# A gated-scan and GELU feed-forward kernel: the second GEMM with its weights stationary and its activations moving

## The chip, the cores and the metric

The kernel runs on one core of one Trainium2 chip. The metric is the device time of one execution in microseconds, smaller is better. Engines: TensorE (PE, its weight loads PEld), VectorE (DVE), ScalarE (ACT), GpSimd (POOL) and SyncE (SP, which here only issues transfers).

## The reference

An attention with a gated running state over 768 time steps for 4 batches of 8 heads of 48, then a feed-forward layer over the 3,072 tokens with 384 features and 2,048 hidden units, all in float32:

```python
for t in range(S):
    state = alpha[:, :, t, :, None] * state + np.einsum('bhd,bhe->bhde', k[:, :, t], v[:, :, t])
    y[:, :, t] = np.einsum('bhd,bhde->bhe', q[:, :, t], state)
...
h = x @ w_in
g = 0.5 * h * (1.0 + erf(h * inv_sqrt2))
return (g @ w_out).astype(np.float32)
```

Here x is y with the heads side by side, w_in is 384 x 2048 and w_out 2048 x 384.

## The kernel before, in words

The tokens are cut into 12 groups of 256 (`G`), three to a batch. For each group the attention part (lines 266 to 535: scans on VectorE, many small TensorE products) makes x transposed, 384 features in three tiles (`NK`) of 128 partitions by 256 tokens, split into a high half `xhi` and a low half `xlo` so that float32r products keep float32's accuracy. The weights are split in the same way (`wih`, `wil`, `woh`, `wol`).

The hidden units are cut into 8 pieces f of 2 x 128. One GEMM1 step (`gemm1`, line 545) makes one piece of one group: for each 128 hidden units j and each feature tile i three products (high by high, high by low, low by high), 18 products of 256 columns with the weights stationary and x moving, into one PSUM tile `hp` of 128 x 512. ScalarE then writes GELU(hp) twice, rounded to float32r as `ghi` (L576) and in full in place (L577), and VectorE writes the difference as `glo` (L582). One GEMM2 step (`gemm2`, line 594) multiplies them with the piece's w_out: for each token half t and each j `ghi` by `woh`, `ghi` by `wol` and `glo` by `woh`, 12 products. There the activations are stationary (a 128 x 128 tile of `ghi` or `glo`) and 384 columns of weights move, into two PSUM tiles `acc0` and `acc1` of 128 tokens x 384. GEMM2 of a piece stands behind GEMM1 of the next piece on TensorE. There are 96 steps of each kind.

After the last piece of a run `evacuate` brings the two accumulators to `part` in SBUF, on ScalarE (L620), VectorE (L622) or, where a group is taken up again, with an add on VectorE (L618). POOL's queue stores it to `out` (L628); the last group alone is stored in two halves from SP's and ScalarE's queues (L624).

The order of the instructions on TensorE, VectorE, ScalarE and SP is made in Python by a planner: a table of costs (`COST`, line 36) and rules give every operation a start, and the operations are then written in the order of the starts (lines 981 to 1022). In the first 380 us the GEMM steps stand between the small products of the attention part; after that there are only GEMM steps. `X_GAP`, `HI_GAP` and `LO_GAP` (line 35) are the sizes in bytes of unused tiles that shift where x, `ghi` and `glo` begin in SBUF.

Of the kernel before, what the change touches and what calls it, by code (L numbers as in the profile page):

```python
# [8 lines left out]
F32 = mybir.dt.float32  # L9
# [6 lines left out]
ALU = mybir.AluOpType  # L16
# [15 lines left out]
RATE, ALONE, LATENCY, SMALL, BEGIN = 350e3, 290e3, 2.1, 50e3, 2.2  # L32
MARGIN = 1.5
HOME = {0: 0, 1: 1, 2: 2, 4: 1, 5: 0, 6: 2, 8: 1, 9: 0, 10: 2, "s": 1}
X_GAP, Z_GAP, HI_GAP, LO_GAP, LATE_GAP = (128, 0, 192), 0, (64, 0), (0, 64), 0
COST = dict(
    scan=0.65, back=0.72, keys=0.65, q=1.35, qv=0.62, scores=1.0, kn=0.5, mask=0.62, inside=1.05, chain=1.15, outer=0.85, carry=0.26, last=0.34, last_p=0.15, sums=0.55, scaled=0.45,
    xh=0.6, xl=0.65, spread=0.62, check=0.95, load=0.46, fetch=0.46, u=0.92, c0=0.56, c1=0.9, c2=0.45, c3=0.95, c4=0.92,
# [6 lines left out]
def gla_then_gelu_ffn(ctx: ExitStack, tc: tile.TileContext, q, k, v, alpha, akq, w_in, w_out, out):  # L45
    nc = tc.nc
    B, H, D, S = q.shape
    NF, P, NK, _ = w_in.shape
    DM, DFF = NK * P, NF * P
    NT = B * S  # L50
    C = 128
    G = 2 * C
# [8 lines left out]
    NG = B * GPB  # L61
    NSB = GPB
# [4 lines left out]
    const = ctx.enter_context(tc.tile_pool(name="const", bufs=1))  # L67
# [5 lines left out]
    ps_o = ctx.enter_context(tc.tile_pool(name="ps_o", bufs=1, space=PSUM))  # L73
# [43 lines left out]
    for t in qk:  # L117
        for h in range(2):
            r = slice(h * DP, (h + 1) * DP)
# [15 lines left out]
    for half in range(2):  # L135
        r = slice(half * CS, (half + 1) * CS)
        nc.gpsimd.affine_select(
            out=mask[r],
# [10 lines left out]
    wi_hi, wi_lo, wo_hi, wo_lo = (  # L149
        [const.tile([P, 2, DM], F32R, name=f"{n}{f2}") for f2 in range(NF2)] for n in ("wih", "wil", "woh", "wol")  # L150
    )
# [28 lines left out]
    for f2 in range(NF2):  # L180
        src = w_in[2 * f2 : 2 * f2 + 2].rearrange("two p c f -> p two (c f)")
        pieces.append((src, wi_hi[f2], wi_lo[f2]))
        src = w_out[2 * f2 * P : (2 * f2 + 2) * P, :].rearrange("(two p) e -> p two e", p=P)
# [303 lines left out]
    def x_tiles(g):  # L487
        if g != "s" and g % (XB + 1) == XB:
            x = late[0].tile([P, NK, 2, G], F32R, tag="xl", name=f"x{g}")
            if g == XB:  # L490
                gap(late[0], LATE_GAP, "gap_late")
        else:
            if g in range(XB):
                gap(ffn, X_GAP[HOME[g]], f"gap_x{g}")
            x = ffn.tile([P, NK, 2, G], F32R, tag=f"x{HOME[g]}", bufs=1, name=f"x{g}")
        xt[g] = x[:, :, 0], x[:, :, 1]
        return x
# [94 lines left out]

        return out

    parts = [const.tile([P, 2, DM], F32, name=f"part{i}") for i in range(NSB)]
    started = set()

    def gemm2(g, f, ghi, glo, acc, first, last, done, n0=None):
        for k in range(2):
            for t in range(2):  # L600
                for j in range(2):
                    for a, w in (((ghi, wo_hi[f]), (ghi, wo_lo[f])), ((glo, wo_hi[f]),))[k]:
                        nc.tensor.matmul(  # L603
                            acc[t],
                            lhsT=a[:, j, t * C : (t + 1) * C],
                            rhs=w[:, j, :],
                            start=(first and j == 0 and k == 0 and w is wo_hi[f]),
                            stop=(last and j == 1 and k == 1),
                        )
        EARLY = tuple(range(NSB))  # L610
        if not last:
            return

        def evacuate():
            o = parts[0 if g == "s" else g % NSB]
            for t in range(2):
                if g in started:
                    nc.vector.tensor_tensor(out=o[:, t], in0=o[:, t], in1=acc[t], op=ALU.add)  # L618
                elif g in EARLY or t == 1 and g == NG - 1:
                    nc.scalar.copy(o[:, t], acc[t])  # L620
                else:
                    nc.vector.tensor_copy(o[:, t], acc[t])  # L622
                if g == NG - 1:
                    (nc.scalar if t else nc.sync).dma_start(out[g * G + t * C : g * G + (t + 1) * C, :], o[:, t])  # L624
            started.add(g)
            if done and g != NG - 1:
                rows = out[g * G : (g + 1) * G, :] if n0 is None else out[bass.ds(n0, G), :]
                nc.gpsimd.dma_start(rows.rearrange("(t p) e -> p t e", p=C), o)  # L628

        return evacuate  # L630

    def general_path():
# [6 lines left out]
        flat = [[x[:, n * NPAIR * G : (n + 1) * NPAIR * G] for n in range(3)] for x in both]  # L639
        st = flat[0][0][:, : DS * D].rearrange("p (d e) -> p d e", e=D)  # L640
# [13 lines left out]
        with tc.For_i(0, S, T) as t0:  # L654
# [20 lines left out]
            half = T * D // 2  # L675
            for i in range(2):
# [3 lines left out]
                    lhsT=sel,  # L680
                    rhs=yc.rearrange("p t e -> p (t e)")[:, i * half : (i + 1) * half],
                    start=True,
                    stop=True,
# [8 lines left out]
        with tc.For_i(0, NT, G) as n0:  # L692
            x_tiles("s")
            xhi, xlo = xt["s"]
            for c in range(2):
                y, z = flat[0][c][:, :DM], flat[1][c][:, :DM].rearrange("p (c h d) -> p c h d", c=NK, h=2)
                nc.sync.dma_start(y, out[bass.ds(n0 + c * C, C), :])
                main, rest = y[:, : NK * DD], y[:, NK * DD :]
                nc.vector.tensor_copy(z[..., :D], main.rearrange("p (c h d) -> p c h d", c=NK, h=2))
                nc.vector.tensor_copy(z[..., D:], rest.rearrange("p (h c d) -> p c h d", c=NK, h=2))  # L700
                xp = small_bank([P, NK, C], f"xp_s{c}")
                for i in range(NK):
                    nc.tensor.transpose(out=xp[:, i, :], in_=z[:, i].rearrange("p h d -> p (h d)"), identity=ident)
                e = slice(c * C, (c + 1) * C)
                nc.scalar.copy(xhi[:, :, e], xp)
                nc.vector.tensor_tensor(out=xlo[:, :, e], in0=xp, in1=xhi[:, :, e].bitcast(F32), op=ALU.subtract)
            acc = [ps_o.tile([P, DM], F32, tag=f"acc{t}", name=f"acc{t}_s") for t in range(2)]
            for f in range(NF2):
                hp = gemm1("s", f)
                gh = gelus("s", f, hp)  # L710
                gl = gelu_low("s", f, hp, gh)
                evacuate = gemm2("s", f, gh, gl, acc, f == 0, f == NF2 - 1, f == NF2 - 1, n0)
            evacuate()
# [180 lines left out]
    def gemm1_op(g, t):  # L894
        f = next_f[g]
        next_f[g] += 1
        st = dict(g=g, f=f, first=g != state["g"], last=False)
        prev = steps[-1] if steps else None
        if st["first"]:
            if prev:  # L900
                prev["last"] = True
                again = prev["g"] >= NSB or prev["g"] in evacuated
                evacuated.add(prev["g"])
                prev["evac"] = Op("DVE" if again else "ACT", "part", lambda p=prev: p["out"](), [prev["gemm2"]], rank=-2)
                waiting[prev["evac"].eng].append(prev["evac"])
            state["run"] += 1
        state["g"] = g
        two = steps[-2] if len(steps) > 1 else {}
        st["gemm1"] = Op("PE", "gemm1", lambda: st.update(hp=gemm1(g, f)))
        st["gelu"] = Op("ACT", "gelu", lambda: st.update(gh=gelus(g, f, st["hp"])), [st["gemm1"], two.get("gemm2")], rank=-3)  # L910
        st["gelu"].cost *= 2
        st["low"] = Op("DVE", "low", lambda: st.update(gl=gelu_low(g, f, st["hp"], st["gh"])), [st["gelu"], two.get("gemm2")], rank=-3)

        if g < NSB and t < UNTIL:
            st["minus"] = Op("PE", "minus", lambda: st.update(rest=gelu_rest(g, f, st["hp"], st["gh"])), [st["gelu"]], rank=-3)
            st["low"] = Op("ACT", "gelu", lambda: st.update(gl=st["rest"]()), [st["minus"], two.get("gemm2")], rank=-2.9)
            waiting["PE"].append(st["minus"])

        def second():
            if st["first"]:  # L920
                st["acc"] = [ps_o.tile([P, DM], F32, tag=f"acc{t}", name=f"acc{t}_{g}_{f}") for t in range(2)]
            else:
                st["acc"] = prev["acc"]
            st["out"] = gemm2(g, f, st["gh"], st["gl"], st["acc"], st["first"], st["last"], f == NF2 - 1)

        st["gemm2"] = Op("PE", "gemm2", second, [st["low"], prev and prev["gemm2"], prev and prev.get("evac")], rank=0)
        waiting["ACT"].append(st["gelu"])
        waiting[st["low"].eng].append(st["low"])
        gemms[g, f] = st["gemm1"]
        steps.append(st)  # L930
        return st["gemm1"]
# [49 lines left out]
    t = 0.0  # L981
    idle = 0
    while True:
        moved = False
        for e in ("DVE", "ACT", "PE", "SP", "POOL"):
            if free_at[e] <= t + 1e-9:
                o = choose(e, t)
# [11 lines left out]
    last = steps[-1]  # L999
# [9 lines left out]
    first = min(o.start for o in plan if o.name == "gemm1")  # L1009
    early = sorted((o for o in plan if o.eng == "PE" and o.start <= first), key=lambda o: o.start)  # L1010
    for o, after in zip(early, early[1:]):
        n = int((after.start - o.end - 0.3) / FILL)
# [18 lines left out]
    with tc.If(rv != 0):  # L1031
        general_path()
# [57 lines left out]
```

## Time and profile before

| | |
|---|---|
| median of 3 runs | 509.78 us (508.96 to 510.25) |
| profiled execution | 510.61 us |
| its span from the first to the last instruction | 509.0 us |
| mean granted TensorE clock | 0.995 |
| TensorE / VectorE / ScalarE / GpSimd busy | 495.7 / 297.3 / 219.6 / 39.1 us |

The profiled execution took 1.6 us more than its span, and 0.83 us more than the median of the runs. Busy time of TensorE counts a moment once where several products overlap, while the duration of a single product in the rows runs from its issue to its modelled end, so that durations of neighbours overlap; how fast products follow one another is read from their starts.

### The profile page before, as it was taken

Reading aid. Unit: us, or ns where it says so; the run is one execution under the profiler, and the core shown is the slowest. Engines: PE = TensorE matmul, PEld = TensorE weight load, DVE = VectorE, ACT = ScalarE, POOL = GpSimd, SP = SyncE. Lnnn points to the kernel's source line nnn. Section 1 sums busy time; section 2 is a strip of 40 time slices with the busy share of each in tenths; the row PEclk is TensorE's granted clock in tenths of the full one; section 3 lists DMA queues with packets and bytes.
Section 4 is the critical chain, followed back from the end, with each engine's and each line's share of the span. In section 5 each row is a group of like instructions: output and inputs, shape, how many; then the busy total and the mean of one; then the engine's idle time right before and its main releaser. Section 6 shows DMA issues by size and latency. Waiting matters only on the chain.

```text
span 509.0 us, 13811 instructions
## 1 busy us (share of the span) xinstructions
PE 495.7 (97%) x5974; PEld 477.0 (94%) x5974; DVE 297.3 (58%) x579; ACT 219.6 (43%) x468; POOL 39.1 (8%) x60
## 2 busy tenths in 40 slices
PE   8898999999999999999999999999999999999995
PEld 7787999999998999999999999999999999999995
DVE  6999899999849968667686267252332211211211
ACT  1676864645544455454453343353323222222221
POOL 4100110100011111121111011010000000000000
PEclk9998999999999999999999999999999999999999
DMA  8957453531033423433332020010000000000001
GB/s 301 381 176 237 184 172 125 186 127 63 1 125 111 136 73 108 133 112 118 109 100 77 0 68 14 1 35 15 1 35 14 0 33 2 32 0 1 32 1 35
DMA packets 15250, 44.20 MB, mean 87 GB/s; under 512 B 2224, under 2 KB 5728, under 8 KB 15184
## 3 DMA queue, kind: packets, MB, share of 16 engines
q1 hardware_dynamic: 13520, 38.44, 22.9%
q0 software_dynamic: 1232, 4.33, 2.2%
q8 instruction: 49, 0.80, 0.7%
q10 hardware_dynamic: 432, 0.49, 0.4%
q14 instruction: 17, 0.14, 0.1%
HBM read 36.18 MB, written 4.72 MB: 80 GB/s over the span
## 4 chain that ended last, share of the span: by engine, by line
PE 80%; issue 12%; ACT 2%; DVE 2%; DMA 2%; POOL 1%; SPq 0%; ACTq 0%; DVEq 0%; POOLq 0%
PE acc L603 34%; PE hp L555 33%; PE s L314 3%; PE ybank L470 3%; PE ybank L387 2%; PE ybank L409 2%; DMA st<-in_moe_w_in_dram 2%; PE spare L1007 1%; ACT junk L170 1%; PE ybank L355 1%; POOL qk L288 1%; PE ybank L533 0%; ACTq L547 0%; SPq L158 0%; ACT L576 0%
## 5 line engine op out<-in xcount | busy, mean ns | idle before, releaser
L555 PE MATMUL hp<-x,wih 128*128 128x256 f32 x1152 | 204.7, 280 | 0.0
L555 PEld LDWEIGHTS hp<-x,wih 128*128 128x128 f32 x1152 | 178.6, 189 | 1.9
L555 PE MATMUL hp<-x,wil 128*128 128x256 f32 x576 | 160.0, 278 | 0.0
L576 ACT ACTIVATE ghi<-hp 128x512 fp32r<-128x512 f32 x96 | 57.4, 598 | 204.8 <-PE hp L555 204.8
L582 DVE TENSOR_TENSOR glo<-hp,ghi 128x512 fp32r<-128x512 f32 x92 | 63.0, 685 | 141.0 <-ACT hp L577 140.9
L603 PE MATMUL acc<-woh,ghi 128*128 128x384 f32 x384 | 131.9, 344 | 0.0
L603 PE MATMUL acc<-wol,ghi 128*128 128x384 f32 x384 | 128.9, 336 | 0.0
L555 PEld LDWEIGHTS hp<-x,wil 128*128 128x128 f32 x576 | 108.9, 189 | 0.0
L603 PE MATMUL acc<-woh,glo 128*128 128x384 f32 x384 | 82.1, 334 | 0.0
L603 PEld LDWEIGHTS acc<-woh,ghi 128*128 128x128 f32 x384 | 72.0, 188 | 3.0
L603 PEld LDWEIGHTS acc<-wol,ghi 128*128 128x128 f32 x384 | 72.1, 188 | 0.0
L603 PEld LDWEIGHTS acc<-woh,glo 128*128 128x128 f32 x384 | 67.9, 188 | 0.0
L577 ACT ACTIVATE hp<-hp 128x512 f32<-128x512 f32 x96 | 56.9, 593 | 0.0
L278 DVE TENSOR_TENSOR_SCAN pp<-akq,top 128x256 f32<-128x256 f32 x48 | 31.3, 680 | 23.5 <-POOL qk L288 21.3
L293 DVE TENSOR_TENSOR_SCAN rp<-akq,rp,top 128x255 f32<-128x255 f32 x48 | 35.2, 762 | 0.7
L288 POOL TENSOR_TENSOR qk<-akq,pp 128x512 f32<-128x512 f32 x18 | 23.7, 1319 | 135.3 <-PE ybank L470 75.5
L628 POOL DMA_DIRECT2D out_dram<-part x11 | 8.4, 762 | 258.6 <-DVE part L622 188.5
L314 PE MATMUL s<-qk,akq 48*64 48x112 f32 x768 | 24.7, 261 | 1.6 <-issue 1.0
L524 ACT CAST x<-ybank 64x256 fp32r<-64x256 f32 (+4 forms) x60 | 20.0, 333 | 11.4 <-PE ybank L470 8.8
L528 DVE TENSOR_TENSOR x<-ybank,x 64x256 fp32r<-64x256 f32 (+3 forms) x54 | 19.2, 355 | 8.5 <-ACT x L524 7.6
L314 PEld LDWEIGHTS s<-qk,akq 48*64 48x64 f32 x768 | 19.4, 133 | 3.8 <-issue 2.8
L323 ACT COPY kn<-s 128x384 f32<-128x384 f32 x24 | 11.6, 482 | 25.0 <-PE s L314 18.1
(78 smaller groups left out, 405.6 us busy)
## 6 DMA issues: line engine op xcount, KB each, us to landing
akq<-in_akq_dram SPq DMA_DIRECT2D x22, 768.0 KB, 4.8
st<-in_moe_w_in_dram SPq DMA_DIRECT2D x8, 768.0 KB, 4.5
st<-in_moe_w_out_dram SPq DMA_DIRECT2D x8, 768.0 KB, 5.2
vn<-in_v_dram SPq DMA_DIRECT2D x12, 384.0 KB, 4.4
out_dram<-part POOLq DMA_DIRECT2D x11, 384.0 KB, 3.2
x<-z SPq DMA_DIRECT2D x63, 32.0 KB, 2.7
akq<-in_akq_dram SPq DMA_DIRECT2D x2, 512.0 KB, 5.5
akq<-in_akq_dram SPq DMA_DIRECT2D x2, 256.0 KB, 2.8
```

Source lines behind the costliest of these rows:

```text
L278: nc.vector.tensor_tensor_scan(pp[:, i], at[:, i], top, MID, ALU.mult, ALU.min)
L288: eng.tensor_tensor(out=qs[:, :, :, :CS], in0=by_chunk(qt), in1=by_chunk(pp), op=ALU.mult)
L293: nc.vector.tensor_tensor_scan(rp[:, i, G - 2 :: -1], at[:, i, G - 1 : 0 : -1], top[:, 1:], rp[:, i, G - 1 :], ALU.mult, ALU.min)
L314: nc.tensor.matmul(d["s"][o, h, e : e + KW], lhsT=d["kt"][r, i, t], rhs=d["qs"][r, i, j], start=True, stop=True)
L470: ins = nc.tensor.matmul(ybank[o, b, t : t + CS], lhsT=states[u][j][r, i], rhs=d["qs"][r, i, j, :CS], start=False, stop=True, skip_group_c ...
L524: nc.scalar.copy(hi, y)
L528: nc.vector.tensor_tensor(out=lo, in0=y, in1=hi.bitcast(F32), op=ALU.subtract)
L555: nc.tensor.matmul(hp[:, j, :], lhsT=a[:, j, i * P : (i + 1) * P], rhs=x[:, i, :], start=(j == 0 and i == 0 and n == 0), stop=(i == NK - 1 ...
L576: nc.scalar.activation(ghi, hp, AF.Gelu)
L577: nc.scalar.activation(hp, hp, AF.Gelu)
L582: nc.vector.tensor_tensor(out=glo, in0=hp, in1=ghi.bitcast(F32), op=ALU.subtract)
L603: nc.tensor.matmul(acc[t], lhsT=a[:, j, t * C : (t + 1) * C], rhs=w[:, j, :], start=(first and j == 0 and k == 0 and w is wo_hi[f]), stop= ...
```

## The change

GEMM2 swaps its operands. A 128 x 128 tile of w_out (`woh` or `wol`, output features i of 128) is now stationary and the 256 tokens of `ghi` or `glo` move, so that a step has 3 output tiles x 2 halves j x 3 terms = 18 products of 256 columns, and the result is transposed: output features on the partitions, tokens along the columns. The accumulators are one PSUM tile of 2 x 256 columns (`acc2`) and one of 256 (`acc1`). The evacuation moves 512 and then 256 columns. The output array holds each block of 256 tokens transposed; the program's last lines turn the blocks round on the host. In the very last step the products are ordered by accumulator, and the two accumulators are copied in halves by VectorE and ScalarE and stored in four transfers. Three gaps change: the x tiles and the weights stay where they were, `ghi` and `glo` begin 64 bytes lower. The planner's costs and rules are untouched.

```diff
-X_GAP, Z_GAP, HI_GAP, LO_GAP, LATE_GAP = (128, 0, 192), 0, (64, 0), (0, 64), 0
+X_GAP, Z_GAP, HI_GAP, LO_GAP, LATE_GAP = (128, 0, 256), 0, (0, 0), (0, 0), 0
...
-    parts = [const.tile([P, 2, DM], F32, name=f"part{i}") for i in range(NSB)]
+    parts = [const.tile([P, NK, G], F32, name=f"part{i}") for i in range(NSB)]
...
+    def accumulators(g, f):
+        return [ps_o.tile([P, n, G], F32, tag=f"acc{n}", name=f"acc{n}_{g}_{f}") for n in (2, NK - 2)]
+
+    def rows_of(start):
+        flat = out[start, :].rearrange("r c -> (r c)")
+        return flat.rearrange("(i p t) -> p i t", p=P, t=G)
+
     def gemm2(g, f, ghi, glo, acc, first, last, done, n0=None):
-        for k in range(2):
-            for t in range(2):
-                for j in range(2):
-                    for a, w in (((ghi, wo_hi[f]), (ghi, wo_lo[f])), ((glo, wo_hi[f]),))[k]:
-                        nc.tensor.matmul(
-                            acc[t],
-                            lhsT=a[:, j, t * C : (t + 1) * C],
-                            rhs=w[:, j, :],
-                            start=(first and j == 0 and k == 0 and w is wo_hi[f]),
-                            stop=(last and j == 1 and k == 1),
-                        )
+        final = done and g == NG - 1
+        terms = ((wo_hi[f], ghi, 0), (wo_lo[f], ghi, 0), (wo_hi[f], glo, 1))
+        todo = [(i, j, n) for i in range(NK) for j in range(2) for n in range(3)]
+        todo.sort(key=lambda x: (x[0] // 2 if final else 0, terms[x[2]][2], x[0], x[1], x[2]))
+        for i, j, n in todo:
+            w, a, k = terms[n]
+            nc.tensor.matmul(
+                acc[i // 2][:, i % 2],
+                lhsT=w[:, j, i * P : (i + 1) * P],
+                rhs=a[:, j, :],
+                start=(first and i % 2 == 0 and j == 0 and n == 0),
+                stop=(last and j == 1 and k == 1),
+                skip_group_check=True,
+            )
...
         def evacuate():
             o = parts[0 if g == "s" else g % NSB]
-            for t in range(2):
+            if final:
+                rows = rows_of(slice(g * G, (g + 1) * G))
+                for b, (i, n) in enumerate(((0, 2), (2, 1))):
+                    to, src = (x.rearrange("p i t -> p (i t)") for x in (o[:, i : i + n], acc[b]))
+                    half = n * G // 2
+                    for k in range(2):
+                        e = slice(k * half, (k + 1) * half)
+                        (nc.scalar.copy if k else nc.vector.tensor_copy)(to[:, e], src[:, e])
+                        at = rows[:, i + k] if n == 2 else rows[:, i, e]
+                        (nc.scalar if k else nc.sync).dma_start(at, to[:, e])
+                return
+            for a, to in zip(acc, (o[:, :2], o[:, 2:])):
                 if g in started:
-                    nc.vector.tensor_tensor(out=o[:, t], in0=o[:, t], in1=acc[t], op=ALU.add)
-                elif g in EARLY or t == 1 and g == NG - 1:
-                    nc.scalar.copy(o[:, t], acc[t])
+                    nc.vector.tensor_tensor(out=to, in0=to, in1=a, op=ALU.add)
+                elif g in EARLY:
+                    nc.scalar.copy(to, a)
                 else:
-                    nc.vector.tensor_copy(o[:, t], acc[t])
+                    nc.vector.tensor_copy(to, a)
...
+    o = got[0].reshape(-1, 384, 256)
+    return o.transpose(0, 2, 1).reshape(got[0].shape)
```

All steps keep their order on every engine; only what stands inside a GEMM2 step and inside an evacuation differs. First TensorE at a GEMM2 step in the last group (group 11, piece 6), behind the last GEMM1 step; a row is line, operation, output<-inputs and shape. Before, the whole step:

```order
L603 MATMUL acc0_11_0_6082<-woh6_160,ghi_11_6_6276 128x384
L603 MATMUL acc0_11_0_6082<-wol6_168,ghi_11_6_6276 128x384
L603 MATMUL acc0_11_0_6082<-woh6_160,ghi_11_6_6276 128x384
L603 MATMUL acc0_11_0_6082<-wol6_168,ghi_11_6_6276 128x384
L603 MATMUL acc1_11_0_6083<-woh6_160,ghi_11_6_6276 128x384
L603 MATMUL acc1_11_0_6083<-wol6_168,ghi_11_6_6276 128x384
L603 MATMUL acc1_11_0_6083<-woh6_160,ghi_11_6_6276 128x384
L603 MATMUL acc1_11_0_6083<-wol6_168,ghi_11_6_6276 128x384
L603 MATMUL acc0_11_0_6082<-woh6_160,glo_11_6_6279 128x384 x2
L603 MATMUL acc1_11_0_6083<-woh6_160,glo_11_6_6279 128x384 x2
```

And with the change, from the seventh product on (the six ahead of it are three more pairs of woh6 and wol6 into acc2):

```order
L612 MATMUL acc2_11_0_6608<-ghi_11_6_6838,woh6_160 128x256
L612 MATMUL acc2_11_0_6608<-ghi_11_6_6838,wol6_168 128x256
L612 MATMUL acc1_11_0_6609<-ghi_11_6_6838,woh6_160 128x256
L612 MATMUL acc1_11_0_6609<-ghi_11_6_6838,wol6_168 128x256
L612 MATMUL acc1_11_0_6609<-ghi_11_6_6838,woh6_160 128x256
L612 MATMUL acc1_11_0_6609<-ghi_11_6_6838,wol6_168 128x256
L612 MATMUL acc2_11_0_6608<-glo_11_6_6841,woh6_160 128x256 x4
L612 MATMUL acc1_11_0_6609<-glo_11_6_6841,woh6_160 128x256 x2
```

Both accumulators take their ghi products first and the glo products stand at the end of the step as before, now as the 13th to the 18th product.

The second place is the end of the program on ScalarE, behind the GELU of the last step. Before:

```order
L576 ACTIVATE ghi_11_6_6276<-hp_11_6_6245 128x512
L577 ACTIVATE hp_11_6_6245<-hp_11_6_6245 128x512
L576 ACTIVATE ghi_11_7_6312<-hp_11_7_6281 128x512
L577 ACTIVATE hp_11_7_6281<-hp_11_7_6281 128x512
L620 COPY part2_175<-acc1_11_0_6083 128x384
L624 DMA out_0_dram<-part2_175 128x384
```

And with the change:

```order
L576 ACTIVATE ghi_11_7_6880<-hp_11_7_6843 128x512
L577 ACTIVATE hp_11_7_6843<-hp_11_7_6843 128x512
L633 COPY part2_175<-acc2_11_0_6608 128x256
L635 DMA out_0_dram<-part2_175 128x256
L633 COPY part2_175<-acc1_11_0_6609 128x128
L635 DMA out_0_dram<-part2_175 128x128
```

One copy of 384 columns and one transfer became a copy and a transfer of half of the first accumulator, and then of half of the second. VectorE and SP's queue have the other halves.

## Rows read from the trace of the kernel before

**Rows 1.** Page, busy us of an engine (share of span) xinstructions.

```profile
PE 495.7 (97%) x5974; PEld 477.0 (94%) x5974; DVE 297.3 (58%) x579; ACT 219.6 (43%) x468; POOL 39.1 (8%) x60
```

**Rows 2.** Page, the chain that ended last: by engine, by line.

```profile
PE 80%; issue 12%; ACT 2%; DVE 2%; DMA 2%; POOL 1%; SPq 0%; ACTq 0%; DVEq 0%; POOLq 0%
PE acc L603 34%; PE hp L555 33%; PE s L314 3%; PE ybank L470 3%; PE ybank L387 2%; PE ybank L409 2%; DMA st<-in_moe_w_in_dram 2%; PE spare L1007 1%; ACT junk L170 1%; PE ybank L355 1%; POOL qk L288 1%; PE ybank L533 0%; ACTq L547 0%; SPq L158 0%; ACT L576 0%
```

**Rows 3.** Waits of TensorE from 60 us on: total us, times, longest.

```profile
PE ybank L387 <- DVE x L528: 1.0, 1, 1.0
```

**Rows 4.** Window from 380 us: us, busy us by engine, PEclk, DMA share, GB/s.

```profile
380.00:497.43 117.43, 117.43 (x859) 117.43 (x858) 24.15 (x40) 31.53 (x58) 2.18 (x3) 1.00 0.04 13
```

**Rows 5.** Timeline of TensorE, late GEMM steps: start us, duration us, line, what.

```profile
377.94 0.34 PE L603 MATMUL acc<-wol,ghi 128*128 128x384 f32 x1
...
378.98 0.33 PE L603 MATMUL acc<-wol,ghi 128*128 128x384 f32 x1
...
386.01 0.39 PE L555 MATMUL hp<-x,wih 128*128 128x256 f32 x2
...
497.43 0.39 PE L555 MATMUL hp<-x,wih 128*128 128x256 f32 x2
```

**Rows 6.** The chain in order of time, pieces of GEMM products: start us, us.

```profile
175.64 2.31 PE hp L555 x18
...
251.81 4.44 PE hp L555 x36
...
263.28 4.08 PE hp L555 x36
...
295.21 2.26 PE hp L555 x18
...
308.39 2.30 PE acc L603 x12
311.28 2.28 PE acc L603 x12
```

**Rows 7.** Timeline of TensorE within the 36 products that begin at 251.74 us.

```profile
252.08 0.28 PE L555 MATMUL hp<-x,wil 128*128 128x256 f32 x1
...
255.97 0.28 PE L555 MATMUL hp<-x,wil 128*128 128x256 f32 x1
```

**Rows 8.** Timeline of VectorE in a late step; in brackets idle time before.

```profile
426.51 0.69 DVE L582 TENSOR_TENSOR glo<-hp,ghi 128x512 fp32r<-128x512 f32 x1 [3.44 <-ACT hp L577]
```

**Rows 9.** Timeline of the program's end, all engines.

```profile
503.49 0.56 DVE L622 COPY part<-acc 128x384 f32<-128x384 f32 x1 [2.01 <-PE acc L603]
503.84 0.48 ACT L620 COPY part<-acc 128x384 f32<-128x384 f32 x1 [3.08 <-PE acc L603]
504.08 0.35 SPq L624 DMA_DIRECT2D out_dram<-part  x1
504.35 0.39 ACTq L624 DMA_DIRECT2D out_dram<-part  x1
```

**Rows 10.** Transfers by issuing queue: count, KB each, median us to landing.

```profile
x<-z SPq DMA_DIRECT2D x63, 32.0 KB, 2.7
...
x<-z ACTq DMA_DIRECT2D x9, 32.0 KB, 4.2
out_dram<-part SPq DMA_DIRECT2D x1, 192.0 KB, 2.2
out_dram<-part ACTq DMA_DIRECT2D x1, 192.0 KB, 3.0
```

**Rows 11.** ScalarE's copies from PSUM by shape: busy us, mean ns, idle before.

```profile
L620 ACT COPY part<-acc 128x384 f32<-128x384 f32 x7 | 3.0, 477 | 3.1 <-PE acc L603 3.1
L524 ACT CAST z<-ybank 128x128 fp32r<-128x128 f32 x9 | 2.4, 266 | 14.3 <-PE ybank L470 14.3
```

**Rows 12.** Timeline of TensorE, f32r products of 512 and of 128 columns.

```profile
64.47 0.39 PE L586 MATMUL hp<-ghi,minus 128*128 128x512 f32 x1
...
64.88 0.38 PE L533 MATMUL ybank<-x,minus 128*128 128x128 f32 x2
65.10 0.45 PE L555 MATMUL hp<-x,wih 128*128 128x256 f32 x2
```

More of the change, by code (lines that the diff above doesn't have):

```diff
@@ L615, in evacuate @@
             o = parts[0 if g == "s" else g % NSB]
-            for t in range(2):
+            if final:
[10 more added lines that the diff above has]
+            for a, to in zip(acc, (o[:, :2], o[:, 2:])):
                 if g in started:
-                    nc.vector.tensor_tensor(out=o[:, t], in0=o[:, t], in1=acc[t], op=ALU.add)
-                elif g in EARLY or t == 1 and g == NG - 1:
-                    nc.scalar.copy(o[:, t], acc[t])
-                else:
-                    nc.vector.tensor_copy(o[:, t], acc[t])
-                if g == NG - 1:
-                    (nc.scalar if t else nc.sync).dma_start(out[g * G + t * C : g * G + (t + 1) * C, :], o[:, t])
+                    nc.vector.tensor_tensor(out=to, in0=to, in1=a, op=ALU.add)
+                elif g in EARLY:
+                    nc.scalar.copy(to, a)
+                else:
+                    nc.vector.tensor_copy(to, a)
             started.add(g)
-            if done and g != NG - 1:
-                rows = out[g * G : (g + 1) * G, :] if n0 is None else out[bass.ds(n0, G), :]
-                nc.gpsimd.dma_start(rows.rearrange("(t p) e -> p t e", p=C), o)
+            if done:
+                nc.gpsimd.dma_start(rows_of(slice(g * G, (g + 1) * G) if n0 is None else bass.ds(n0, G)), o)
         return evacuate
@@ L706, in general_path @@
                 nc.vector.tensor_tensor(out=xlo[:, :, e], in0=xp, in1=xhi[:, :, e].bitcast(F32), op=ALU.subtract)
-            acc = [ps_o.tile([P, DM], F32, tag=f"acc{t}", name=f"acc{t}_s") for t in range(2)]
+            acc = accumulators("s", 0)
             for f in range(NF2):
@@ L920, in second @@
             if st["first"]:
-                st["acc"] = [ps_o.tile([P, DM], F32, tag=f"acc{t}", name=f"acc{t}_{g}_{f}") for t in range(2)]
+                st["acc"] = accumulators(g, f)
             else:
@@ L1088 @@
     got = tuple(r.results[0][f"out_{i}_dram"] for i in range(len(_OUTS)))
-    return got[0]
+    o = got[0].reshape(-1, 384, 256)
+    return o.transpose(0, 2, 1).reshape(got[0].shape)
```

## The prediction

> **What bounds the kernel now.** I read the engine totals first. TensorE is busy 97% of the span, VectorE 58%, ScalarE 43% [rows 1]. The chain that ended last is 80% TensorE, and its two largest lines are the two GEMMs, L603 with 34% and L555 with 33% [rows 2]. Then I asked for what TensorE waited for from 60 us on: one wait of 1.0 us in 449 us [rows 3]. [...] So from about 60 us on a nanosecond saved or added in a GEMM product reaches the end. The question is what a product costs, and for that the start of one product to the start of the next counts, not its listed duration, since products overlap.
>
> *The period of two steps.* I call the 18 products of one (group, pair of 128-wide d_ff blocks) in the first GEMM a GEMM1 step, and its 12 products in the second a GEMM2 step. GEMM1 steps start at 386.01 and 497.43 us with 27 steps of each kind between them [rows 5]: 111.42 / 27 = 4.127 us for one of each. Two GEMM1 steps back to back take 4.08 us for 36 products [rows 6], so 113.3 ns for 256 columns and 2.040 us a step. A GEMM2 step is then 4.127 - 2.040 = 2.087 us. Inside one, products 2 and 8 start at 377.94 and 378.98 us [rows 5]: 173.3 ns for 384 columns. [...]
>
> *A second rhythm.* The reader should see two kinds of GEMM1 in the chain: 36 products in 4.08 us and 36 products in 4.44 us [rows 6]. In the second kind products 3 and 36 start at 252.08 and 255.97 us [rows 7], 33 products in 3.89 us, 117.9 ns each and steady to the last one. It begins only where GEMM1 follows the small products of the attention part, and not always: of 14 such pieces in the chain from 150 to 400 us ten are slow (like 2.31 us for 18, 4.44 for 36), four fast (like 2.26). It costs 4.5 ns a product, 0.08 us a step. Every GEMM1 step behind a GEMM2 step runs at 113.3, whatever its x tile and weights.
>
> **The change part by part.**
>
> *18 products of 256 for 12 of 384.* The columns are the same, 4,608 a step. The new product has the form of GEMM1's: a 128x128 weight tile loaded, 256 activation columns moving, result to half a PSUM bank. I take GEMM1's 113.3 ns: 18 x 113.3 = 2.040 us, 0.047 less than 2.087. For the 65 GEMM2 steps that follow another GEMM step this is 65 x 0.047 = 3.1 us. The other 31 follow small products (24 of them in the chain from 150 us on) and take 2.28 to 2.30 us [rows 6]; GEMM1 steps in that place take 2.26 in the fast rhythm and 2.31 in the slow one. Weighted ten to four that is 2.30, so I book no gain there; all fast or all slow would give -1 or +1 us.
>
> [...]
>
> *Operands change sides.* The weight load now takes woh and wol, which were ready long before, and ghi and glo move. Nothing waits today for ghi or glo: VectorE had stood idle for 3.44 us before the glo row at 426.51 us [rows 8], and TensorE waited for neither [rows 3]. GEMM2's first product with glo is its 13th, 12 x 113.3 = 1.36 us into the step, as against 8 x 173.3 = 1.39 now. Cost nothing. Without the idle 3.4 us it would be the 0.69 us of that row a step.
>
> *Gaps.* They move ghi and glo by 64 bytes and leave x and the weights in place. No row shows a price; GEMM1 reads x tiles at several places at the same 113.3, so I book nothing. The bound is the slow rhythm, 4.5 ns a product.
>
> *Evacuation.* 512 and 256 columns for twice 384, the same columns in the same number of instructions; VectorE and ScalarE have room, and the next GEMM2 step comes a GEMM1 step (2.04 us) later. Nothing. The output transfers on POOL's queue move the same bytes in 384 pieces for 256, under later groups.
>
> *The end.* Today ScalarE copies the last 384 columns from 503.84 us in 0.48 us and its queue issues the last transfer at 504.35 [rows 9], which lands 3.0 us later [rows 10]. The new last step finishes the first bank six products (0.68 us) earlier; 128 columns a side are left, 0.27 us by the nearest rows for 0.48 [rows 11]. ScalarE must first finish 256 columns and an issue, about 0.1 us too long for those 0.68. The last transfer is 64 KB for 192; those of 32 KB land in 2.7 on SP's queue and 4.2 on ScalarE's [rows 10]. So -0.6 to +1.1 us; I take -0.3, since the 4.2 stands for transfers in the crowded early part. SP's queue gets one transfer more; nothing stands behind it.
>
> *Sum.* The profiled execution took 510.61 us (509.0 of span and 1.6 around it): 510.6 - 3.1 - 0.3 = 507.2. The median of the runs is 0.83 us lower, so 506.4.
>
> **The rivals.**
>
> *A: the slow rhythm outlives the step it starts in (slower).* Today the wide products end it: no GEMM1 step behind a GEMM2 step is slow. With 256 columns everywhere nothing wide is left, and what starts behind small products may hold until the next small products. For it: it held through all three pieces of 36 slow products that I see (4.44 us). Against it: four of the 14 pieces lose it by themselves early in the step (2.26 us), and no fast run was seen to turn slow. Price: a GEMM1 step loses 0.08, a GEMM2 step 2.12 - 2.087 = 0.03 us and its gain of 0.047, 0.16 us a pair. The forecast's 3.4 us are gone at 21 pairs. The last run alone has 30 pairs: +4.8 us, 511.2. All runs slow: about 65 GEMM2 and 70 GEMM1 steps, 65 x 0.08 + 70 x 0.08 = +10.8 us, 517.2. In ten of 14 runs: 514.
>
> [...]
>
> *C: little changes.* If the slow rhythm lasts only through the short runs between 150 and 360 us (about 37 GEMM2 and 40 GEMM1 steps, ten in 14 slow: 4.4 us), the gain is used up: 510.8.
>
> **How the numbers follow.** A measurement of this kernel can tell about 0.3% (1.5 us) from no change. Forecast 506.4, with 504.6 (entries fast, end at its best) to 508.2: 0.58. C and A's smaller half, 508.3 to 511.3: 0.14. A's larger part, 511.3 to 517: 0.21. B: 0.05, and 0.02 for what I don't see. Faster 0.60, same 0.14, slower 0.26. The range 504.6 to 514 leaves out some 2 in 10, most of it above.
>
> **What would show it.** Right: in the last 120 us a period of 4.08 us for a GEMM1 and a GEMM2 step, products 113.3 ns apart in both, and some 4 us less from 60 us to the last product. Wrong by A: 117.9 ns in GEMM1 steps behind GEMM2, a period of 4.24. [...] The end is right if the last transfer is issued about 0.2 us sooner behind the last product.

## The result: slower by 0.9%

The changed kernel takes 513.62 us (median of 5 runs, 513.51 to 515.40) against 509.78 (5 runs, 508.23 to 510.25): ratio 1.0090, 95% interval 1.0067 to 1.0114. The forecast was 506.4 us and faster; the time lies inside its range, close to the upper end (514.0), where rival A stood. The profiled execution took 513.62 us with a span of 512.0, against 510.61 and 509.0.

The page of the kernel after answers to [rows 1, 2]; first the busy time of the engines, then the chain that ended last, by engine and by line.

```profile
PE 499.0 (97%) x6550; PEld 483.3 (94%) x6550; DVE 297.7 (58%) x580; ACT 219.8 (43%) x469; POOL 40.7 (8%) x60
...
PE 78%; issue 12%; DVE 8%; POOL 1%; ACT 1%; ACTq 0%; DVEq 0%; POOLq 0%
PE acc L612 33%; PE hp L555 33%; PE s L314 3%; PE ybank L470 2%; PE ybank L387 2%; PE ybank L409 2%; PE warm L89 2%; DVE pp L278 1%; DVE st L243 1%; DVE w L212 1%; DVE ss L328 1%; DVE rp L293 1%; DVE wil L253 1%; DVE u L225 1%; POOL qk L288 1%
```

Nothing here tells the loss: TensorE is as full as before, and the two GEMMs (L612 is the second, L555 the first) hold a third of the chain each, as before. The waits of TensorE from 60 us on are as in [rows 3], one of 1.1 us for 1.0:

```profile
PE ybank L387 <- DVE x L528: 1.1, 1, 1.1
```

So no wait took the place of anything; products themselves came farther apart. As in [rows 5], the timeline of TensorE gives the starts of GEMM1 steps. The first row below is the step that began at 65.10 in the kernel before [rows 12], the other two are those at 386.01 and 497.43.

```profile
63.20 0.45 PE L555 MATMUL hp<-x,wih 128*128 128x256 f32 x2
...
385.30 0.40 PE L555 MATMUL hp<-x,wih 128*128 128x256 f32 x2
...
499.77 0.40 PE L555 MATMUL hp<-x,wih 128*128 128x256 f32 x2
```

From the second to the third lie 27 steps of each kind: 114.47 / 27 = 4.240 us a pair, where it was 4.127 and the forecast said 4.08. That is the 4.24 named for rival A. The window between them (total, busy us of PE, PEld, DVE, ACT, POOL, granted clock, DMA share, GB/s) has TensorE busy all the time at clock 1.00, like [rows 4]:

```profile
385.30:499.77 114.47, 114.47 (x974) 114.47 (x973) 21.73 (x33) 29.38 (x54) 2.29 (x3) 1.00 0.03 12
```

The chain in order of time (start us, us, what), which answers to [rows 6], shows where the rhythm changes:

```profile
356.33 2.25 PE acc L612 x18
358.59 2.04 PE hp L555 x18
360.63 2.04 PE acc L612 x18
...
376.78 2.32 PE acc L612 x18
379.10 4.24 PE hp L555 x36
383.34 2.12 PE acc L612 x18
385.46 2.12 PE hp L555 x18
...
497.82 2.12 PE acc L612 x18
```

The run that starts at 356 us does what was forecast: 2.04 us for a step of either GEMM, 113.3 ns a product. The run from 376.78 to the last product stands at 2.12 us in every step of both GEMMs, 117.8 ns a product. I call the two spacings the fast and the slow rhythm, as in the forecast, and a stretch of GEMM steps between two stretches of small products a run. In this kernel each run takes one of the two within its first step and keeps it. Counted over the starts of all products of the trace: of the 65 GEMM2 steps behind another GEMM step 21 are fast and 44 slow; of the 74 such GEMM1 steps 19 are fast and 55 slow, where before three were slow.

**The account.** From the step at 65.10 to that at 497.43 the kernel before took 432.33 us, the kernel after 436.57: +4.24. The steps give it: 21 x -0.047 = -1.0; 44 x (2.12 - 2.087) = +1.5; 55 - 3 = 52 GEMM1 steps x 0.08 = +4.2; the first steps of runs give back some 0.4. From there to the issue of the last transfer it is 6.92 us before [rows 5, 9] and 7.48 after, +0.56, of which 0.15 are slow steps. The start, up to 63 us, was 1.9 us shorter. That is scatter: in the run of e7 below, whose instructions are the same up to the last run, the same step began at 66.23. The rest of the span's +3.0 is 0.1 from that issue to the end.

### The profile page after: what moved, and what is told of

Same layout as the page of the kernel before. It is cut to its first block, busy times and chain, and to the rows that moved or that the text cites. A ratio compares the mean times of both kernels' runs of the same rounds, so it can differ in the third digit from the quotient of the medians.

```text
span 512.0 us, 14969 instructions
## 1 busy us (share of the span) xinstructions
PE 499.0 (97%) x6550; PEld 483.3 (94%) x6550; DVE 297.7 (58%) x580; ACT 219.8 (43%) x469; POOL 40.7 (8%) x60
## 4 chain that ended last, share of the span: by engine, by line
PE 78%; issue 12%; DVE 8%; POOL 1%; ACT 1%; ACTq 0%; DVEq 0%; POOLq 0%
PE acc L612 33%; PE hp L555 33%; PE s L314 3%; PE ybank L470 2%; PE ybank L387 2%; PE ybank L409 2%; PE warm L89 2%; DVE pp L278 1%; DVE st L243 1%; DVE w L212 1%; DVE ss L328 1%; DVE rp L293 1%; DVE wil L253 1%; DVE u L225 1%; POOL qk L288 1%
## 5 line engine op out<-in xcount | busy, mean ns | idle before, releaser
L555 PE MATMUL hp<-x,wih 128*128 128x256 f32 x1152 | 207.4, 281 | 0.0
L555 PEld LDWEIGHTS hp<-x,wih 128*128 128x128 f32 x1152 | 175.5, 189 | 1.8
L555 PE MATMUL hp<-x,wil 128*128 128x256 f32 x576 | 160.9, 279 | 0.0
L612 PE MATMUL acc<-ghi,woh 128*128 128x256 f32 x576 | 141.7, 285 | 0.0
L612 PE MATMUL acc<-ghi,wol 128*128 128x256 f32 x576 | 138.4, 279 | 0.0
L612 PEld LDWEIGHTS acc<-ghi,woh 128*128 128x128 f32 x576 | 108.5, 188 | 3.0
L612 PEld LDWEIGHTS acc<-ghi,wol 128*128 128x128 f32 x576 | 108.7, 189 | 0.0
L555 PEld LDWEIGHTS hp<-x,wil 128*128 128x128 f32 x576 | 108.3, 188 | 0.0
L612 PE MATMUL acc<-glo,woh 128*128 128x256 f32 x576 | 82.6, 279 | 0.0
L612 PEld LDWEIGHTS acc<-glo,woh 128*128 128x128 f32 x576 | 73.9, 189 | 0.0
## 6 DMA issues: line engine op xcount, KB each, us to landing
akq<-in_akq_dram SPq DMA_DIRECT2D x2, 512.0 KB, 4.7
```

The source lines that it names most:

```text
L555: nc.tensor.matmul(hp[:, j, :], lhsT=a[:, j, i * P : (i + 1) * P], rhs=x[:, i, :], start=(j == 0 and i == 0 and n == 0), stop=(i == NK - 1 ...
L612: nc.tensor.matmul(acc[i // 2][:, i % 2], lhsT=w[:, j, i * P : (i + 1) * P], rhs=a[:, j, :], start=(first and i % 2 == 0 and j == 0 and n ...
```

## The experiments

Times are medians; each ratio is against runs of the kernel before on the same chip, with its 95% interval.

### Does a wide product end the slow rhythm? (e1)

```diff
+        if run["new"]:      # first GEMM1 step of a run of six steps or more
+            nc.tensor.matmul(hp, lhsT=wi_hi[f][:, 0, :P], rhs=xw[g][:, 0], start=True, stop=True, ...)
```

A product of 512 columns into hp, which the step's own first product overwrites.

> One f32r product of 512 columns (its result is overwritten by the next product, so the output stays as it is) stands ahead of the first GEMM1 step in each of the six runs of six or more GEMM steps. Theory A (the rhythm is fixed where a run begins, and only a product of another width ends it): behind the wide product all products are 113.3 ns apart, the last run of 61 steps has a period of 4.08 us in place of 4.24; gain 59 x 0.08 there, about 21 x 0.08 in the three other slow long runs, cost 6 x 0.23: 513.6 - 6.4 + 1.4 = 508.6. Theory B (the place of the operands makes the products slow): the period stays 4.24 and the time grows by 1.4 to 515.0.

Measured: 515.77 us, ratio 1.0137 (1.0102 to 1.0171). What theory A expected failed; the period of the last run stayed as theory B had it and the time is near its 515.0; B's reason, the places, is tested further down. The chain of e1 at the last run (L557 is the added product):

```profile
379.21 2.32 PE acc L621 x18
381.52 0.23 PE hp L557
381.76 4.24 PE hp L564 x36
386.00 2.12 PE acc L621 x18
```

Slow ahead of the wide product and slow behind it. Elsewhere the run at 278 us, slow in the kernel after, came out fast, and the run at 107 us, fast there, came out slow. Two more wide products stood within a run: at 89.38 us with slow products ahead of it and fast ones behind, at 354.01 us with fast ones ahead and slow ones behind. Of the stretches behind the six wide products two are fast and four slow. So a wide product did not as a rule end the slow rhythm here; behind it the rhythm came out either way. So the forecast's reason for the fast GEMM1 steps of the kernel before ("the wide products end it") falls too.

### Can a narrow product end it? (e2, e7)

```diff
-                    nc.tensor.matmul(hp[:, j, :], ..., rhs=x[:, i, :], ...)
+                    for e in halves_of((j, i, n) == (1, 0, 1)):   # (0:128), (128:256) once in a run
+                        nc.tensor.matmul(hp[:, j, e], ..., rhs=x[:, i, e], ...)
```

The first step of a run has one product of 256 columns cut into two of 128 (its 11th product if it is a GEMM1 step, its 10th if a GEMM2 step): e2 in 13 of the 14 runs of three steps or more (the run at 356 us has no cut and was fast without one), e7 in the last run alone, where only one product was cut and not the two that its expectation speaks of.

> In the first step of each of the 13 runs of three or more GEMM steps one product in the middle (the 11th of a GEMM1 step, the 10th of a GEMM2 step) is done as two of 128 columns, the same work. Theory A: any product of another width will do, so products behind it are 113.3 ns apart; gain 60 x 0.08 in the last run, some 28 x 0.08 in the other long ones and 10 x 0.08 in those of three, cost 13 x 0.11: 513.6 - 7.8 + 1.4 = 507.2. If a narrow product does not do what a wide one does, products stay 117.9 apart and the time is 515. Theory B: 515.

> The kernel after, with one product of 256 columns split in two of 128 in the first step of GEMM1 and one in the first step of GEMM2 of the last run of steps only (61 steps, 376 to 506 us). Theory A: the last run turns to 113.3 ns behind the splits and gives back 60 steps by 0.08 us less 0.1 for the splits: 4.7 us, so 508.9 us; the other runs stay as in the kernel after. Rival (the rhythm is no property of a run but of the whole execution, or the gain of e2 came from the short runs): 512 us or more.

Measured: e2 507.94 us, ratio 0.9972 (0.9958 to 0.9986), now faster than the kernel before. e7 509.81 us, ratio 1.0006 (0.9994 to 1.0018); from the first to the last product of the last run 124.6 us where the kernel after has 129.3, so -4.7 as expected. The median is 0.9 us above the expected 508.9: e7's ten executions spread from 508.47 to 511.99, and in the profiled one, the slowest of them, the last run began 3.2 us later than in the kernel after (379.91 for 376.71). Where the median's 0.9 us lie, one profile does not show. The timeline of TensorE in e2 at the start of the last run:

```profile
377.39 0.28 PE L622 MATMUL acc<-ghi,wol 128*128 128x256 f32 x1
377.50 0.28 PE L622 MATMUL acc<-ghi,woh 128*128 128x256 f32 x1
377.62 0.33 PE L622 MATMUL acc<-ghi,wol 128*128 128x128 f32 x2
377.79 0.34 PE L622 MATMUL acc<-ghi,woh 128*128 128x256 f32 x1
377.96 0.28 PE L622 MATMUL acc<-ghi,wol 128*128 128x256 f32 x1
...
378.78 0.39 PE L564 MATMUL hp<-x,wih 128*128 128x256 f32 x2
379.01 0.28 PE L564 MATMUL hp<-x,wil 128*128 128x256 f32 x1
379.12 0.39 PE L564 MATMUL hp<-x,wih 128*128 128x256 f32 x2
```

(A row "x2" is two products.) Ahead of the cut the starts are some 118 ns apart; the cut product takes 0.17 us to the next; from 378.78 to 379.12 three products take 0.34 us, and it stays at 113.3 to the end. Behind the cut all 13 runs were fast; nine of them were slow ahead of it, four were fast already. One turned slow again in its middle, at this place of e2; the first row is VectorE's evacuation of the accumulators:

```profile
132.59 1.01 DVE L649 TENSOR_TENSOR part<-part,acc 128x512 f32<-128x512 f32 x2
...
133.05 0.39 PE L564 MATMUL hp<-x,wih 128*128 128x256 f32 x2
133.27 0.28 PE L564 MATMUL hp<-x,wil 128*128 128x256 f32 x1
133.42 0.35 PE L622 MATMUL acc<-ghi,woh 128*128 128x256 f32 x1
133.61 0.28 PE L622 MATMUL acc<-ghi,wol 128*128 128x256 f32 x1
```

Two products there start 0.15 and 0.19 us behind the one ahead of them instead of 0.11, and the rest of that run, this step and three more, goes at 117.8. The first of the two writes the accumulator that VectorE is emptying: the first of VectorE's two adds ends at 133.27 us, the product starts 0.15 us later. In e9 (below), which has the same cuts, the add ends at 133.21, the same product starts at 133.35, and the same run turns slow; in the kernel after the add is done 0.55 us ahead of the product, and that run stays fast. So in e2 and e9 the rhythm was taken anew at this place, and in the kernel after, e2, e7, e9 and e11 no other run changed its rhythm behind its first step.

### What did the gaps do? (e3, e4)

```diff
 e3, in the kernel after:
-X_GAP, Z_GAP, HI_GAP, LO_GAP, LATE_GAP = (128, 0, 256), 0, (0, 0), (0, 0), 0
+X_GAP, Z_GAP, HI_GAP, LO_GAP, LATE_GAP = (128, 0, 192), 0, (64, 0), (0, 64), 0
 e4, in the kernel before: the other way round
```

In the compiled programs this moves nothing but the four buffers of the GELU halves, by 64 bytes. I give the place of a buffer in a partition as the remainder of its address by 256: all weights stand at 32, all x tiles at 224, the halves at 32 with the old gaps and at 224 with the new.

> The changed kernel with the gaps of before, one part of the change undone: ghi and glo lie 64 bytes higher. Theory A: each run still holds one rhythm from its second step on, 113.3 or 117.9 ns, drawn at its start; the time lies between 505 (all fast) and 517 (all slow), most of it set by the last run. Theory B: with the gaps of before GEMM2's products change all alike, whichever run they are in.

> The kernel before with the changed kernel's gaps. Theory A: GEMM1 steps behind GEMM2 steps stay at 113.3 ns since the wide products reset them, 509.8 within 1 us. Theory B: the new places of ghi and glo slow GEMM2's or GEMM1's products, some 3 us or more.

Measured: e3 514.90 us, ratio 1.0115 (1.0088 to 1.0143); e4 514.85 us, ratio 1.0107 (1.0080 to 1.0135). The forecast booked nothing for the gaps; for the old form of the GEMM they are worth 1.1%. The chain in the last run, e3 first, then e4:

```profile
442.21 2.06 PE hp L555 x18
444.27 2.14 PE acc L612 x18
446.41 2.06 PE hp L555 x18
```

```profile
440.70 2.09 PE acc L603 x12
442.79 2.12 PE hp L555 x18
444.91 2.09 PE acc L603 x12
```

In e3 the products of GEMM2 come 120.0 ns apart in every run (from the ninth of a step on; those ahead of it take 112 to 120, so that a step is 2.14 us), and GEMM1, whatever it did at the start of a run, is fast in all 74 steps behind another GEMM step. In e4 the wide products keep their 173.3 ns, and GEMM1 is slow in 73 of those 74 steps, where the same program with the halves 64 bytes further on has 71 fast. The x tiles and the weights of GEMM1 lie where they did, so its rhythm hangs on where the operands of the other GEMM lie. Form and place belong together:

| | halves at 32 | halves at 224 |
|---|---|---|
| 12 products of 384 | 509.8: GEMM1 2.04, GEMM2 2.087 | 514.85: GEMM1 2.12, GEMM2 2.09 |
| 18 products of 256 | 514.9: GEMM1 2.06, GEMM2 2.14 | 513.6: both 2.04 or both 2.12, by run |

### Which places? (e5, e6, e8, e10, e12, e13)

All are the kernel after with other gaps and nothing else; the fence leaves out the changes of `X_GAP` that keep the x tiles in place, and in e10 one gap more that leaves x of the groups 3, 7 and 11 at 224.

```diff
 e5:  +    gap(const, 32, "gap_all")            # moves all but x of the groups 3, 7 and 11
 e6:  HI_GAP, LO_GAP = (128, 0), (0, 128)       # halves at 96
 e8:  HI_GAP, LO_GAP = (192, 0), (0, 192)       # halves at 160
 e12: HI_GAP, LO_GAP = (32, 0), (0, 32)         # halves at 0
 e13: HI_GAP, LO_GAP = (224, 0), (0, 224)       # halves at 192
 e10: X_GAP, HI_GAP, LO_GAP = (192, 0, 64), (192, 0), (0, 192)   # x at 32, halves at 224
```

> The kernel after, with 32 bytes of gap ahead of the buffers, so that the weights, the x tiles and the GELU halves all begin at a multiple of 64 bytes in a partition instead of 32 bytes behind one; their places relative to each other stay (the profiles of e3 and e4 showed that 64 bytes more or less for the GELU halves alone decide the spacing of products). Theory A (the rhythm of a run is drawn at its start and is held; the place matters only relative to other operands): products of 113.3 or 117.8 ns as before, about 513.6 us, 508 to 516 by what is drawn. [...]

> The kernel after, with the four GELU-half buffers 128 bytes further on (96 instead of 224 bytes behind a multiple of 256; weights at 32 and x at 224 stay). Theory A with the finding of e3 (halves at the weights' place, 32, make each product of the second GEMM 120.0 ns, and leave the first GEMM fast): products of the second GEMM at 113.3 or 117.8, the rhythm drawn anew at each run; 508 to 516 us by the draws, a third value excluded. Rival P (each place has a spacing of its own, nothing is drawn): one spacing of the second GEMM in all runs, another than with halves at 224, and one spacing of the first GEMM behind it; 120.0 in all would give 514.9 as in e3.

> As the run with halves at 96, with the halves at 160 bytes behind a multiple of 256. Theory A: 508 to 516 us by the draws, both rhythms found in one execution. Rival P: one spacing in all runs of steps, whatever stands ahead of them.

> The mirror of e3: the kernel after with the x tiles of the groups 0 to 2, 4 to 6 and 8 to 10 moved to 32 bytes behind a multiple of 256, where the weights stand, and the GELU halves left at 224 (the x tiles of the groups 3, 7 and 11 stay at 224 too). Theory M (what a product takes depends on where its moving operand stands against its weights): the first GEMM of the moved groups at 120.0 ns a product, that of the groups 3, 7 and 11 at 113.3 or 117.8, the second GEMM at 113.3 or 117.8: 72 steps by 0.04 to 0.12 us more than in the kernel after and whatever the second GEMM gives back, 512 to 519 us. Rival (only the place of the GELU halves matters, since they alone are written while they are read): first GEMM unchanged, 508 to 516 us with no step at 120.0.

> The kernel after with the four GELU-half buffers 32 bytes further on, at a multiple of 256 bytes in a partition (weights at 32, x at 224). Theory M (spacing set by where the moving operand stands against its weights; halves at another place than x, so that the two GEMMs go each at a spacing of its own): second GEMM at one spacing in nearly all steps, first GEMM at 113.3 or 117.8. If 32 bytes behind 224 reads like 224: second GEMM 113.3 or 117.8, 507 to 514 us. If like the weights' own place (32, 32 bytes on): 120.0, 514 to 517 us. Rival (only steps of 64 bytes matter, 0 reads as 224): the rhythm of a run held through both GEMMs as in the kernel after, 508 to 516 us.

> The kernel after with the four GELU-half buffers 32 bytes nearer to the start of a line, at 192 bytes behind a multiple of 256. Theory M: a spacing of the second GEMM between those of 160 (118.6) and 224 (113.3 or 117.8), each GEMM at its own, 511 to 517 us. Rival (192 reads as 224): the rhythm of a run held through both GEMMs, the last run at 117.8 in all its steps, 513 to 514 us.

| | us, ratio (interval) | GEMM2, ns a product | GEMM1, ns a product |
|---|---|---|---|
| e5, 32 on | 514.90, 1.0112 (1.0089 to 1.0136) | 113.3 or 117.8 (two steps 115) | 113.3 or 117.8 (groups 3, 7, 11: 117.4 or 118.8) |
| e6, halves 96 | 515.99, 1.0125 (1.0099 to 1.0151) | 117.8 | 113.3 or 117.8 |
| e8, halves 160 | 516.60, 1.0141 (1.0118 to 1.0164) | 118.4 to 118.9 | 113.3 or 117.8 |
| e10, x 32 | 514.20, 1.0097 (1.0076 to 1.0118) | 113.3 in 63 of 65 steps | 120.0 (groups 3, 7, 11: 113.3 or 117.8) |
| e12, halves 0 | 517.38, 1.0182 (1.0157 to 1.0208) | 117.8 to 118.6 | 113.3 or 117.8 |
| e13, halves 192 | 515.88, 1.0147 (1.0128 to 1.0165) | 117.4 or 118.8 | 113.3 or 117.8 |

The spacings are those of steps behind another GEMM step: 113.3, 117.8 and 120.0 as a step settles, the others as its mean. e10 is the mirror of e3 and shows both of its places within one run, where the groups change; its chain:

```profile
326.53 2.14 PE hp L557 x18
328.67 2.06 PE acc L614 x18
330.73 2.04 PE hp L557 x18
332.77 2.04 PE acc L614 x18
```

The GEMM1 step at 326.53 moves an x tile at 32, the weights' place, the one at 330.73 (group 3) one at 224: 2.14 and 2.04 us. Of the 72 steps of the moved groups 71 settle at 120.0 ns (one in the early stretch is slower still), of the 24 others none.

e5 did not move everything: the x tiles of the groups 3, 7 and 11 are laid out from the other end of the memory and stayed at 224, while weights, halves and the other x tiles went on by 32 bytes. That makes it two tests. Where weights and moving operand went on together, both GEMMs kept their two rhythms; the halves then stand at 0, and e12 with the halves at 0 and the weights left at 32 never has GEMM2 at 113.3. So in these runs it is the distance that counts and not the place itself. And where only the weights went on, the distance shrank from 192 to 160 bytes, the distance that e13 gives to GEMM2 by moving the halves. The chain of e5 at two GEMM1 steps of group 3, then that of e13 at a GEMM2 step:

```profile
193.38 4.27 PE hp L556 x36
```

```profile
331.68 2.13 PE acc L612 x18
```

Of the 19 such GEMM1 steps of e5 four have a mean of 117.4 ns and 15 one of 118.6 to 118.8; of e13's 65 GEMM2 steps 25 one of 117.4 and 40 one of 118.6 to 118.8. The single starts agree too: the step of e5 at 193.22 us and that of e13 at 406.13 both go 117, 120, 118, 119, 117, 121, 120, 116 ns. With e3 and e10, where a distance of 0 gave 120.0, this shows that in this kernel the place of the moving operand against its weights decides which spacings a product can have, whichever of the two operands is moved. It does not decide which of the two rhythms a run takes at a distance of 192 bytes; e4 shows that the other GEMM has a part in that. Of the distances tried, none but 192 let GEMM2 go at 113.3 ns for long. The runs show such places and distances alone; the line that e13's expectation speaks of was assumed, and no run shows one.

### The end of the program (e11, e9)

```diff
-                    for k in range(2):   # two copies and two transfers for each bank, in halves
-                        ...
+                nc.vector.tensor_copy(o[:, :2], acc[0]); nc.sync.dma_start(rows[:, :2], o[:, :2])
+                nc.scalar.copy(o[:, 2:], acc[1]); nc.scalar.dma_start(rows[:, 2:], o[:, 2:])
```

The timeline of the end in the kernel after, which answers to [rows 9], and its transfers (count, KB each, median us to landing), which answer to [rows 10]; [rows 11] had 477 and 266 ns for the copies of 384 and 128 columns, the second fits:

```profile
505.63 0.42 DVE L633 COPY part<-acc 128x256 f32<-128x256 f32 x1 [1.72 <-PE acc L612]
506.09 0.37 ACT L633 COPY part<-acc 128x256 f32<-128x256 f32 x1 [2.90 <-DVE part L633]
506.33 0.29 DVE L633 COPY part<-acc 128x128 f32<-128x128 f32 x1 [0.28 <-PE acc L612]
506.96 0.27 ACT L633 COPY part<-acc 128x128 f32<-128x128 f32 x1 [0.50 <-DVE part L633]
507.25 0.34 ACTq L635 DMA_DIRECT2D out_dram<-part  x1
...
out_dram<-part ACTq DMA_DIRECT2D x1, 64.0 KB, 2.6
```

Both of ScalarE's copies were released by VectorE's copy out of the same accumulator, not by TensorE: the two halves of an accumulator were copied one after the other, the first ending at 506.05 us and the second beginning at 506.09. The last transfer is issued 1.23 us behind the start of the last product; before it was 0.89.

> The kernel after with that end of the program alone (one copy and one transfer on each of the two engines). If the end is what the copies set: 0.4 to 0.5 us off 513.6, so 513.2 us; from the last product to the end of the span 5.5 us where the kernel after has 6.0. If the landing of transfers sets it: 6.0 us again.

> The kernel of e2 (one product of 256 columns split in two of 128 near the start of each run of three steps or more), and at the end of the program one copy of two token blocks on VectorE with one transfer, one copy of the last block on ScalarE with one transfer, in place of two copies and two transfers each. In the kernel after, ScalarE's copy of 128x256 starts at 506.09 where VectorE's ends, and its 128x128 at 506.96 behind VectorE's 128x128 and 0.75 us behind the last product; with one copy on each engine the last transfer is issued some 0.4 to 0.5 us earlier. Theory A: 507.9 of e2 less 0.4: 507.5 us, 507.0 to 508.2, so 0.3 to 0.4% under the kernel before. Rival (the end is set by when the transfers land, not by the copies): 507.9 as e2; a transfer of 128 KB more than one of 64 KB would show as a later end.

The end in e11:

```profile
505.60 0.69 DVE L628 COPY part<-acc 128x512 f32<-128x512 f32 x1 [1.72 <-PE acc L612]
506.30 0.37 ACT L630 COPY part<-acc 128x256 f32<-128x256 f32 x1 [3.15 <-PE acc L612]
506.32 0.40 SPq L629 DMA_DIRECT2D out_dram<-part  x1
506.70 0.39 ACTq L631 DMA_DIRECT2D out_dram<-part  x1
```

Now each engine reads an accumulator of its own, as in the kernel before, and both still write into one tile: ScalarE waits for TensorE alone. The last issue comes 0.71 us behind the last product, and the span ends 5.3 us behind it instead of 6.0 (e9: 5.3, e2: 5.8). In the time this cannot be seen: e11 513.78 us, ratio 1.0093 (1.0071 to 1.0114), where 513.2 was expected; e9 508.02, ratio 0.9981 (0.9970 to 0.9991), no different from e2. The traces show 0.5 to 0.7 us, the medians nothing; that stays open. e2 and e9, both some 0.2 to 0.3% under the kernel before, are the fastest versions found.

## Why the prediction was wrong

**The step that failed** is "I take GEMM1's 113.3 ns" for 65 GEMM2 steps, with GEMM1's own steps left at 2.040. Forecast: -3.1 us for the first and 0 for the second. Measured: 21 of the 65 at 2.04, 44 at 2.12, together +0.5; and 52 more GEMM1 steps at 2.12, +4.2. It was the second that turned the sign, and it came with the gaps: with the halves back at 32 bytes GEMM1 is fast in all 74 such steps of the new form (e3), and with the halves at 224 it is slow in 73 of 74 of the old (e4). Rival A had this and priced it rightly: 0.16 us a pair, 4.24 for the period, the last run alone 4.8 us (e7: 4.7 given back by one cut product in that run). It was given 0.21 and a share of 0.14. The evidence put against it, that four of 14 pieces lose the slow rhythm early in a step and none turns slow, was right as seen but did not bear on it: early is when a run takes its rhythm, and after that it keeps it.

**The reason given for the fast GEMM1 steps of before was wrong.** It was not the width of the products between them: with the same wide products and the halves at 224 instead of 32, GEMM1 is slow in 73 of 74 steps (e4), and a still wider product did not end the slow rhythm of the last run (e1).

**The gaps were booked at nothing**, from GEMM1's 113.3 ns at several x places; but those x tiles all have the same remainder, 224, so the trace of before held no evidence on places at all. Nor would leaving the gaps alone have saved the forecast, since GEMM2 then pays (e3: 514.9 us). The price, 64 bytes of the halves alone: +1.1% for the old form, and 120.0 ns a product of GEMM2 in the new form if they are not moved. The bound taken, 4.5 ns a product, was the right one for e4; e3's 120.0 is 6.7 over the fast rhythm. The 0.05 of the chance given to B stood for a loss that comes with every product of GEMM2 whatever its width. No run shows such a term: the runs showed the same product of 256 columns at 113.3, 117.8 or 120.0 ns, by its place and by the run it stands in, and with the old gaps a GEMM2 step of 2.14 us (e3).

**Right:** a fast step of GEMM2 is 2.04 us; first steps take 2.25 or 2.32 (forecast 2.26 or 2.31) and cancel; operands that changed sides, evacuation and output transfers cost nothing, since TensorE's waits did not change (one of 1.1 us for one of 1.0). **The end** was mis-sized: -0.3 forecast, some +0.4 measured in the trace, because ScalarE's copy, from 506.09 us, waited for VectorE's out of the same accumulator, which ended at 506.05; the forecast reckoned the two side by side.

**Open:** what decides which rhythm a run takes at its start. Mere chance it is not: of the 13 runs of three steps or more ahead of the last one, 12 took the same rhythm in the profiles of the kernel after, e7 and e11, whose instructions are the same up to there. Open too: why a product of 128 columns set the fast one in 13 runs of 13 and one of 512 columns in two of six; whether the remainder by 256 is the right measure of a place. Not tried: the weights moved by themselves for GEMM2, or by other steps than 32 bytes.

## What to carry to other kernels

Where TensorE is the bound and does nothing but products, read the distance between starts in every run of products, not a mean: two or three spacings can stand in one program, and 64 bytes in the place of one GEMM's operand can change the spacing of the other (e4). Do not take a spacing from one GEMM to another whose operands lie elsewhere: try a buffer 64 bytes further on, and measure form and place together, since here each alone cost about 1% (e3, e4) and both together no more. One product cut in two near the start of the last run cost 0.1 us (e7: it and the next product took 0.34 us, where two took 0.24), and the run was 4.7 us shorter with it.

## What the runs showed of the hardware

The same f32r product (128x128 weights loaded for it, 256 columns moving) came 113.3, 117.8 or 120.0 ns apart. In the kernel after 113.3 and 117.8 both stand between 276.00 and 376.70 us at a granted clock of 1.00, and TensorE waited once from 60 us on, for 1.1 us. The mean clock of the executions with 120.0 was 0.998 (e3) and 0.994 (e10). 120.0 was found where the moving operand had the same remainder by 256 bytes as its weights, whichever GEMM it was (e3, e10). At a distance of 160 bytes steps had means of 117.4 or 118.6 to 118.8, whichever GEMM and whichever operand was moved (e5, e13). At 192 bytes it had two spacings, 113.3 and 117.8, and a stream kept either behind its first step for up to 60 steps, about 1,080 products (117.8 in the kernel after, 113.3 in e7).

These runs do not show what lies behind the spacings. The place of one operand against the other was worth 6.7 ns a product: 120.0 for GEMM2 in e3 and for GEMM1 of the moved groups in e10, 113.3 at a distance of 192 bytes in the fast rhythm.
